# Sigmoid attention, ELU layer and expert choice on one core: batch 0's attention takes two chunks in one stretch of TensorE

## The chip, the cores and the metric

The kernel runs on one core of a Trainium2 chip. Five engines each run their own list of instructions in order and wait for one another through semaphores: TensorE (PE, with its weight loads as PEld), VectorE (DVE), ScalarE (ACT), GpSimd (POOL) and SyncE (SP), whose queue issues nearly all the transfers. The metric is the device time of one launch in microseconds (us); less is better.

## The reference

Four batches of sigmoid attention, an ELU layer and an expert-choice layer, one after the other:

```
q, k, v: (4, 12, 448, 64)
scores = q @ k.T / sqrt(64) - log(448)
x = (1 / (1 + exp(-scores))) @ v             # to (1792, 768)
h = x @ w_in                                 # (768, 2048)
x = where(h > 0, h, exp(min(h, 0)) - 1) @ w_out   # to (1792, 768)
# expert choice: 8 experts, 224 tokens each, by sorted gate logits
out[mask] = relu(x[mask] @ w1[e]) @ w2[e]
```

w_in and w_out come as 64-bit floats, the other inputs that matter here as 32-bit floats.

## The kernel before, in words

Every product of two fp32 matrices that must be exact is split: an operand x is held as h (rounded to the matmul format fp32r) and l = x - h, and three matmuls h\*h, h\*l, l\*h are added up. An operation on VectorE or ScalarE makes h (a copy, `hcopy`), and one on VectorE makes l (a subtraction, `lsub`).

**Attention** of a batch (`attention(b)`) goes by pairs of heads, six in a batch, and by chunks of 112 keys, four in a pair: 24 chunks. `scores(n)` is six matmuls of 64 rows into one of two twin tiles of PSUM, which are taken in turn (`twin_74` for even chunks, `twin_75` for odd ones in the order rows below). ScalarE then writes the sigmoid of the whole twin into a buffer `ad[n]`. `values(n)`, two matmuls with 64 output rows each, adds the chunk to the pair's sum in the one bank `bank_73`. `values` of a chunk comes `XLA` = 2 chunks after its scores. After a pair's fourth chunk the sum is split into h and l (`xs[b]`), and the next pair's first `values` has to wait for that, since it writes the same bank.

**Layer 1** (`layer1(b)`) computes, for each of 16 column blocks f of w_in, 18 matmuls of 128x128x448 (six row blocks c, one for each pair of heads, by three products) into one of three banks in turn (`bank_70` to `bank_72`). The block's ELU is two operations on ScalarE (exp and tanh), two on VectorE, and a split of the result. The second of the two on VectorE is the last that reads the bank. **Layer 2** (`layer2(b)`) adds 16 such blocks for each of six columns d of w_out, in two banks in turn (`bank_70`, `bank_71`), so that its first matmul needs `bank_70`, which block f = 15 held.

**Weights.** In batch 0, `weights` loads each block as 64-bit words into one of two arena tiles (`arena<-w_in`, 768 KB) and `join` makes 32-bit floats of it: one operation on ScalarE that reads the arena, then three on VectorE (`TENSOR_SCALAR`, and two `SCALAR_TENSOR_TENSOR` that read the arena). The joined block goes to memory for the later batches (`wcopy`) and is split into h and l; h and l have three buffers each.

**Order.** The order of instructions on every engine is fixed when the kernel is built, by a list scheduler (`Plan`). Each call adds an operation with a priority and modelled cost; `plan.unit()` binds several matmuls into one operation that nothing comes between; `plan.run()` then places operations one at a time on the engine where the model has the earliest start, and copies (`AV_`) go to ScalarE or VectorE as the model prefers. At run time each engine keeps its list, whatever the real times are, and so does SP's queue with its transfers.

Of the kernel before, what the change touches and what calls it, by code (L numbers as in the profile page):

```python
# [37 lines left out]
Z1R = 11648  # L38
FMAX = 3.4028234663852886e38
W0 = 11  # L40
AC0 = 1
AC1 = 2


# [246 lines left out]
def kernel(  # L291
# [34 lines left out]
    plan = Plan(nc)  # L326
# [62 lines left out]
    def hcopy(dst, src):  # L389
        AV_.copy(dst, src)  # L390

    def lsub(dst, src, h):
        V.tensor_tensor(out=dst, in0=src, in1=f32(h), op=ALU.subtract)
# [126 lines left out]
    def prep(g, st):  # L520
        x, vr = pairs[g]
        h, l = r_kqh(), r_kql()
        for c in (slice(0, S), slice(S, 2 * S)) if g == 0 else (slice(0, 2 * S),):
            hcopy(h[:, c], x[:, c])
            lsub(l[:, c], x[:, c], h[:, c])
        st[g] = (h[:, :S], l[:, :S], h[:, S:], l[:, S:], vr)
        load_pair(g + 2)

    def attention(b):


        st, ad = {}, {}
        n0, n1 = b * HP * C, (b + 1) * HP * C
        AC = AC0 if b == 0 else AC1
        acc = {}

        def scores(n):
            g, c = divmod(n, C)
            kh, kl, qh, ql, _ = st[g]
            ps = sc()  # L540
            for i, (w, m) in enumerate(((kh, qh), (kh, ql), (kl, qh))):
                for j in range(2):
                    o = slice(j * D, (j + 1) * D)
                    PE.matmul(ps[:CP, j, :S], w[o, c * CP:(c + 1) * CP], m[o], start=i == 0, stop=i == 2)
            return ps

        def values(n):
            g, c = divmod(n, C)
            if c == 0:
                acc[g] = av()  # L550
            v, s = st[g][4], ad.pop(n)
            for j in range(2):
                o = slice(j * D, (j + 1) * D)
                PE.matmul(acc[g][o, :S], v[:, c, o], s[:, j], start=c == 0, stop=c == C - 1)

        for n in range(n0, n1 + XLA, AC):
            new = [i for i in range(n, n + AC) if i < n1]
            old = [i for i in range(n - XLA, n - XLA + AC) if i >= n0]
            for i in new:
                g, c = divmod(i, C)  # L560
                if i == n0:
                    prep(g, st)
                if c == PP and g + 1 < (b + 1) * HP:
                    prep(g + 1, st)
            with plan.unit():
                pss = [scores(i) for i in new]
                if b:
                    for i in old:
                        values(i)
            if not b and old:  # L570
                with plan.unit():
                    for i in old:
                        values(i)
            for i, ps in zip(new, pss):
                ad[i] = r_s()[:CP]
                A.activation(ad[i], ps[:CP, :, :S], AF.Sigmoid, bias=bias_s[:CP], scale=QS)
            if old and old[-1] % C == C - 1:
                h, l = r_xH(), r_xL()
                ps = acc.pop(old[-1] // C)
                hcopy(h, ps[:, :S])  # L580
                lsub(l, ps[:, :S], h)
                xs[b].append((h, l))
# [104 lines left out]
    V.tensor_scalar(ident, pj, 0.0, None, op0=ALU.is_equal)  # L687
    plan.bias = BIAS[0]
    attention(0)
    for b in range(B):  # L690
        plan.bias = BIAS[1] if b == 0 else {}
        layer1(b)
        if b == 0:
            plan.dma(wg, w_gate.rearrange("(d p) e -> p d e", p=P))
            V.tensor_copy(wgs[:, :, :E], wg)
            lsub(wgs[:, :, E:], wg, wgs[:, :, :E])
            V.memset(wgp, 0.0)
            V.tensor_copy(wgp[:, :, :E], wg)
        plan.bias = BIAS[2] if b == 0 else {}
        if b + 1 < B:  # L700
            attention(b + 1)
        layer2(b)
# [403 lines left out]
```

## Time and profile before

| what | value |
| --- | --- |
| time, median of 3 runs | 1009.49 us (1008.43 to 1009.92) |
| the profiled execution's own time | 1010.62 us |
| its span, first to last instruction | 1008.8 us |
| PE busy | 976.4 us (97%) |
| DVE busy | 752.6 us (75%) |
| ACT busy | 445.8 us (44%) |
| DMA queue q1, share of 16 engines | 48.8% |

Busy is the time in which an engine ran instructions of work. The shares are means over a program of several stages: attention of batch 0 fills the first 48 us, its layer 1 runs to 121 us, beside the start of batch 1's attention, and the rest follows. A row of the timeline gives start, duration, engine, operation, result and operands, how many instructions were merged, and in brackets the idle time before with what ended it. The trace counts a `values` matmul as two.

### The profile page before, as it was taken

How to read it: one execution, taken by the hardware profiler on the slowest of the kernel's cores; microseconds unless marked ns; L12 is line 12 of the kernel's file. 1: busy time of each engine (PE TensorE's matmuls, PEld its weight loads, DVE VectorE, ACT ScalarE, POOL GpSimd, SP SyncE). 2: the span in 40 equal slices, each digit the busy share in tenths (PEclk: the TensorE clock that was granted, in tenths of full speed). 3: DMA queues.
4: the chain of work that ended last, by engine and by line, in shares of the span. 5: the costliest groups of instructions: out<-in, count | busy, mean ns of one | idle time of the engine just before them, and what ended most of it. 6: DMA issues, size and time to landing. Idle time of an engine off the chain costs nothing. (4 is left out here: it accounts for less than half of the span.)

```text
span 1008.8 us, 15529 instructions
## 1 busy us (share of the span) xinstructions
PE 976.4 (97%) x6039; PEld 811.5 (80%) x6039; DVE 752.6 (75%) x1335; ACT 445.8 (44%) x631; POOL 45.6 (5%) x42
## 2 busy tenths in 40 slices
PE   8999999998999999899999999999899999999997
PEld 3497666786886698777678898888899989989997
DVE  5899977769996445997434687788798899798861
ACT  6779856446564412675320342133433244342320
POOL 0000000000000000000000000010011111102000
PEclk9999999999999999999999999999899999999999
DMA  7856767866452366433124333375555547456820
GB/s 218 294 201 237 264 229 265 271 230 213 175 203 86 115 171 198 164 115 111 63 79 138 113 115 105 120 252 185 174 208 174 187 137 278 163 168 239 282 89 28
DMA packets 63562, 177.99 MB, mean 176 GB/s; under 512 B 6336, under 2 KB 28096, under 8 KB 60416
## 3 DMA queue, kind: packets, MB, share of 16 engines
q1 hardware_dynamic: 60832, 165.98, 48.8%
q0 software_dynamic: 2656, 11.01, 3.5%
q8 instruction: 47, 0.77, 0.3%
q14 instruction: 27, 0.22, 0.1%
HBM read 147.87 MB, written 29.10 MB: 175 GB/s over the span
## 5 line engine op out<-in xcount | busy, mean ns | idle before, releaser
L247 PE MATMUL bank<-zone_r 128*128 128x448 f32 (+1 forms) x3384 | 633.7, 343 | 12.9 <-DVE zone L247 10.1
L247 PEld LDWEIGHTS bank<-zone_r 128*128 128x128 f32 x3384 | 556.3, 191 | 79.5 <-issue 20.6
L247 DVE TENSOR_TENSOR zone_r<-zone,zone_r 128x768 fp32r<-128x768 f32 (+3 forms) x347 | 314.3, 918 | 34.9 <-ACT zone_r L247 28.3
L247 PE MATMUL twin<-zone_r 128*112 128x384 f32 (+2 forms) x1416 | 226.2, 354 | 3.3 <-ACT zone L247 3.3
L247 PEld LDWEIGHTS twin<-zone_r 128*112 128x112 f32 (+2 forms) x1416 | 187.0, 175 | 33.4 <-issue 15.6
L247 ACT ACTIVATE zone_r<-zone 128x768 fp32r<-128x768 f32 (+3 forms) x194 | 151.6, 795 | 123.2 <-PE bank L247 48.6
L247 ACT ACTIVATE zone<-bank 128x448 f32<-128x448 f32 x156 | 79.5, 542 | 187.2 <-PE bank L247 161.0
L247 DVE CAST zone_r<-zone 128x768 fp32r<-128x768 f32 (+3 forms) x153 | 84.9, 557 | 91.0 <-PE bank L247 69.5
L247 ACT ACTIVATE zone<-twin,bias_s 112x896 f32<-112x896 f32 x96 | 92.8, 1005 | 61.5 <-PE twin L247 61.2
L247 PE MATMUL bank<-zone 112*64 112x448 f32 x384 | 83.9, 553 | 0.9 <-DVE zone_r L247 0.9
L247 ACT ACTIVATE zone_r<-bank 128x448 fp32r<-128x448 f32 x62 | 33.5, 544 | 111.5 <-PE bank L247 111.2
L247 DVE SCALAR_TENSOR_TENSOR zone<-arena,zone 128x768 int32<-128x768 int32 (+1 forms) x56 | 59.8, 1068 | 1.0
L247 PEld LDWEIGHTS bank<-zone 112*64 112x64 f32 x384 | 22.8, 136 | 37.7 <-issue 33.8
L247 DVE TENSOR_TENSOR arena<-m,arena 128x896 bf16<-128x896 f32 (+1 forms) x35 | 51.0, 1457 | 0.0
L247 ACT ACTIVATE zone<-twin 112x384 f32<-112x384 f32 (+2 forms) x48 | 24.7, 536 | 50.3 <-DVE zone L247 20.0
L247 DVE SCALAR_TENSOR_TENSOR zone<-zone 128x448 f32<-128x448 f32 x64 | 39.5, 618 | 2.5 <-ACT zone L247 2.5
L247 DVE SCALAR_TENSOR_TENSOR zone<-zone,bank 128x448 f32<-128x448 f32 x64 | 39.4, 616 | 1.0
L891 POOL DMA_INDIRECT zone<-x2rows,idx x18 | 24.2, 1343 | 340.6 <-PE bank L247 234.8
L247 ACT ACT_TABLE_LOAD x29 | 37.2, 1283 | 3.3 <-PE bank L247 1.6
L247 DVE CAST zone_r<-bank 128x448 fp32r<-128x448 f32 x13 | 8.1, 623 | 36.1 <-PE bank L247 36.1
L247 DVE TENSOR_TENSOR zone_r<-bank,zone_r 128x448 fp32r<-128x448 f32 x45 | 27.5, 618 | 3.1 <-ACT zone_r L247 2.7
L247 ACT ACTIVATE zone<-arena 128x768 f32<-128x768 f32 (+1 forms) x28 | 28.1, 1004 | 2.2 <-DMA arena<-w_out 1.3
(106 smaller groups left out, 365.9 us busy)
## 6 DMA issues: line engine op xcount, KB each, us to landing
zone<-we SPq DMA_DIRECT2D x64, 768.0 KB, 5.7
zone<-wcopy SPq DMA_DIRECT2D x48, 384.0 KB, 3.0
zone<-wcopy SPq DMA_DIRECT2D x36, 512.0 KB, 3.3
arena<-w_in SPq DMA_DIRECT2D x16, 768.0 KB, 4.7
arena<-w_out SPq DMA_DIRECT2D x12, 1024.0 KB, 5.9
arena<-w_outT SPq DMA_DIRECT2D x12, 1024.0 KB, 7.1
x2rows<-zone SPq DMA_DIRECT2D x48, 224.0 KB, 3.8
zone<-kq SPq DMA_DIRECT2D x23, 448.0 KB, 3.4
```

The costliest lines, as they stand in the source:

```text
L247: fn = lambda: getattr(self.eng[e], name)(*args, **kw)
L891: plan.add([("G", 1.05, lambda: plan.eng["G"].indirect_dma_start(**kw))], [plan.region(x) for x in reads], [plan.region(x) for x in writes ...
```

## The change

`attention` takes AC = 2 chunks a step in batch 0 as well, where it took one; and the values of the two older chunks go into the same unit as the scores of the two new ones, where they had a unit of their own.

```
-AC0 = 1
 AC1 = 2
...
-        AC = AC0 if b == 0 else AC1
+        AC = AC1
...
             with plan.unit():
                 pss = [scores(i) for i in new]
-                if b:
-                    for i in old:
-                        values(i)
-            if not b and old:
-                with plan.unit():
-                    for i in old:
-                        values(i)
+                for i in old:
+                    values(i)
```

Since the list scheduler starts from other units, the order on every engine changes up to some 260 us of the program. Three places follow; in them `zone`, `zone_r` and `arena` are buffers, and x6 is six instructions in a row.

ScalarE, from the sigmoid of chunk 3 on (`zone<-twin,bias_s` is a sigmoid, even chunks from twin_74; `zone<-arena_77` is ScalarE's part of the join of w_in block 0). Before:

```order
L247 ACTIVATE zone<-twin_75,bias_s 112x896
L247 ACTIVATE zone<-twin_74,bias_s 112x896
L247 ACTIVATE zone<-twin_75,bias_s 112x896
L247 ACTIVATE zone_r<-bank_73 128x448
L247 ACTIVATE zone<-twin_74,bias_s 112x896
L247 ACTIVATE zone<-twin_75,bias_s 112x896
L247 ACTIVATE zone<-twin_74,bias_s 112x896
L247 ACTIVATE zone<-arena_77 128x768
L247 ACTIVATE zone<-twin_75,bias_s 112x896
```

The same stretch of ScalarE now, from the sigmoid of chunk 3 to that of chunk 10:

```order
L246 ACTIVATE zone<-twin_75,bias_s 112x896
L246 ACTIVATE zone<-twin_74,bias_s 112x896
L246 ACTIVATE zone<-twin_75,bias_s 112x896
L246 ACTIVATE zone<-twin_74,bias_s 112x896
L246 ACTIVATE zone<-arena_77 128x768
L246 ACTIVATE zone<-twin_75,bias_s 112x896
L246 ACTIVATE zone_r<-zone 128x768
L246 ACTIVATE zone<-twin_74,bias_s 112x896
L246 ACTIVATE zone<-twin_75,bias_s 112x896
L246 ACTIVATE zone<-twin_74,bias_s 112x896
```

The join stood behind the sigmoid of chunk 8 and now stands behind that of chunk 6, ahead of chunk 7's; the split of the attention's first sum (`zone_r<-bank_73`) has left ScalarE for VectorE, and the copy of the joined weights (`zone_r<-zone`) now stands ahead of the sigmoid of chunk 8.

SP's queue from the transfer of the fifth pair's v and of w_in block 0 on. Before:

```order
L278 DMA zone<-vP 112x512
L278 DMA arena_77<-w_in 128x1536
L278 DMA zone<-kq 128x896
L278 DMA zone<-vP 112x512
L278 DMA arena_78<-w_in 128x1536
L278 DMA wcopy<-zone 128x768
```

And now:

```order
L277 DMA zone<-vP 112x512
L277 DMA arena_77<-w_in 128x1536
L277 DMA zone<-kq 128x896
L277 DMA wcopy<-zone 128x768
L277 DMA zone<-vP 112x512
L277 DMA arena_78<-w_in 128x1536
```

The write-back of the joined block 0 has come ahead of the load of block 1; in both orders that load stands behind v of the sixth pair.

TensorE between the last values of batch 0's attention (`bank_73`) and block f = 7 of layer 1 (18 matmuls into one of bank_70 to bank_72 are one block f). Before:

```order
L247 MATMUL bank_73<-zone 64x448 x8
L247 MATMUL bank_70<-zone_r 128x448 x15
L247 MATMUL bank_71<-zone_r 128x448 x18
L247 MATMUL bank_72<-zone_r 128x448 x18
L247 MATMUL bank_70<-zone_r 128x448 x18
L247 MATMUL bank_71<-zone_r 128x448 x18
L247 MATMUL bank_72<-zone_r 128x448 x18
L247 MATMUL bank_70<-zone_r 128x448 x18
L247 MATMUL bank_71<-zone_r 128x448 x18
```

And now, where 45 of the 54 matmuls of blocks 0 to 2 stand among the attention's chunks already:

```order
L246 MATMUL bank_73<-zone 64x448 x4
L246 MATMUL twin_74<-zone_r 112x448 x6
L246 MATMUL twin_75<-zone_r 112x448 x6
L246 MATMUL bank_70<-zone_r 128x448 x3
L246 MATMUL bank_71<-zone_r 128x448 x3
L246 MATMUL bank_72<-zone_r 128x448 x3
L246 MATMUL twin_74<-zone_r 112x448 x6
L246 MATMUL twin_75<-zone_r 112x448 x6
L246 MATMUL bank_73<-zone 64x448 x4
L246 MATMUL bank_70<-zone_r 128x448 x18
L246 MATMUL bank_71<-zone_r 128x448 x18
L246 MATMUL bank_72<-zone_r 128x448 x18
```

The last pair of heads' share of blocks 0 to 2 and the first four chunks of batch 1 stand ahead of block 3 now. From here to the first matmul of layer 2 the old order holds five pairs of scores and four pairs of values of batch 1, the new one four and three. Counted over the whole program, TensorE's list falls from 466 stretches of matmuls of one shape to 457.

## Rows read from the trace of the kernel before

**Rows 1.** Three stretches: busy us (instructions) of each engine, granted clock, DMA share, GB/s
```profile
0.00:57.70 57.70, 53.09 (x300) 27.03 (x301) 39.24 (x70) 41.05 (x50) 0.43 (x5) 1.00 0.79 257
57.70:128.30 70.60, 65.21 (x333) 50.94 (x331) 68.38 (x101) 59.11 (x84) 0.00 (x0) 1.00 0.67 228
128.30:160.00 31.70, 31.61 (x166) 22.89 (x166) 22.95 (x27) 19.36 (x22) 0.00 (x0) 0.95 0.69 242
```

**Rows 2.** Timeline of VectorE at two of the ELUs of layer 1
```profile
53.21 0.55 DVE L247 TENSOR_SCALAR zone<-zone 128x768 int32<-128x768 int32 x1
...
55.67 0.62 DVE L247 SCALAR_TENSOR_TENSOR zone<-zone 128x448 f32<-128x448 f32 x1
56.20 0.95 DVE L247 TENSOR_TENSOR zone_r<-zone,zone_r 128x768 fp32r<-128x768 f32 x1
57.07 0.61 DVE L247 SCALAR_TENSOR_TENSOR zone<-zone,bank 128x448 f32<-128x448 f32 x1
...
127.72 0.62 DVE L247 SCALAR_TENSOR_TENSOR zone<-zone,bank 128x448 f32<-128x448 f32 x1
```

**Rows 3.** Timeline of TensorE, the start of layer 2
```profile
128.39 8.51 PE L247 MATMUL bank<-zone_r 128*128 128x448 f32 x33 [2.68 <-DVE zone L247]
```

**Rows 4.** Timeline of TensorE in and behind batch 0's attention
```profile
6.48 1.48 PE L247 MATMUL twin<-zone_r 64*112 64x448 f32 x12
...
13.55 0.87 PE L247 MATMUL twin<-zone_r 64*112 64x448 f32 x6
...
15.25 1.49 PE L247 MATMUL twin<-zone_r 64*112 64x448 f32 x12
16.68 1.72 PE L247 MATMUL bank<-zone 112*64 112x448 f32 x8
18.33 0.86 PE L247 MATMUL twin<-zone_r 64*112 64x448 f32 x6
...
20.81 0.97 PE L247 MATMUL bank<-zone 112*64 112x448 f32 x4
...
23.01 0.87 PE L247 MATMUL twin<-zone_r 64*112 64x448 f32 x6 [0.44 <-ACT zone L247]
...
48.27 29.39 PE L247 MATMUL bank<-zone_r 128*128 128x448 f32 x141
```

**Rows 5.** Timeline of SP's queue: transfers issued
```profile
15.36 0.33 SPq L278 DMA_DIRECT2D zone<-vP  x1
15.74 0.42 SPq L278 DMA_DIRECT2D arena<-w_in  x1
...
21.82 0.33 SPq L278 DMA_DIRECT2D zone<-vP  x1
22.20 0.42 SPq L278 DMA_DIRECT2D arena<-w_in  x1
25.07 0.33 SPq L278 DMA_DIRECT2D wcopy<-zone  x1
```

**Rows 6.** Timeline of ScalarE around its first join
```profile
16.23 1.91 ACT L247 ACTIVATE zone<-twin,bias_s 112x896 f32<-112x896 f32 x2 [0.26 <-PE twin L247]
19.29 1.01 ACT L247 ACTIVATE zone<-twin,bias_s 112x896 f32<-112x896 f32 x1 [1.16 <-PE twin L247]
21.16 0.90 ACT L247 ACTIVATE zone<-arena 128x768 f32<-128x768 f32 x1 [0.86 <-DMA arena<-w_in]
21.96 0.99 ACT L247 ACTIVATE zone<-twin,bias_s 112x896 f32<-112x896 f32 x1
```

**Rows 7.** Timeline of ScalarE behind batch 0's attention
```profile
51.46 0.84 ACT L247 ACTIVATE zone_r<-zone 128x768 fp32r<-128x768 f32 x1 [2.52 <-PE bank L247]
52.21 0.91 ACT L247 ACTIVATE zone<-arena 128x768 f32<-128x768 f32 x1
53.14 1.28 ACT L247 ACT_TABLE_LOAD   x1
54.43 0.98 ACT L247 ACTIVATE zone<-bank 128x448 f32<-128x448 f32 x2
```

**Rows 8.** Who TensorE waited for between 6 and 48 us: us, times, longest
```profile
PE twin L247 <- ACT zone L247: 0.9, 2, 0.5
PE bank L247 <- DVE zone_r L247: 0.9, 2, 0.5
```

**Rows 9.** TensorE alone, 2 us each: busy us, granted clock, DMA share, GB/s
```profile
126.00:128.00 2.00, 0.00 (x0) 1.00 0.55 191
130.00:132.00 2.00, 2.00 (x7) 0.50 0.97 317
```

## The prediction

> **What bounds the kernel now.** I read the page's busy shares first: TensorE is busy 97% of the span, so at first sight anything that shortens its list shortens the program. But the change touches only the first stages, so I split those with the view by stretches [rows 1]. Its second stretch, from the release of layer 1's block 0 to that of block 15, shows VectorE busy 68.38 of 70.60 us and TensorE 65.21: there VectorE sets the pace. The two ends of this stretch are the second and third of the ELU rows on VectorE that matter: the operation that last reads block 0's bank starts at 57.07 and ends at 57.7, and block 15's starts at 127.72 and ends at 128.3 [rows 2]. Layer 2's first matmul starts at 128.39, right behind it, after 2.68 us in which TensorE waited for VectorE [rows 3]; it needs the bank that block 15 held. From there TensorE is busy 31.61 of 31.70 us [rows 1]. So the chain is: batch 0's attention, then VectorE's joins and ELUs up to 128.3, then TensorE. A gain on TensorE ahead of 128 us reaches the end only if VectorE comes sooner, and what TensorE leaves undone there is paid later in full. In the first stretch VectorE is busy 39.24 of 57.70 us; those 18.5 us of idle time are what can grow or shrink.
>
> **The stretches saved.** A chunk alone takes TensorE 1.70 us (13.55 to 15.25) and two chunks in one stretch 3.08 (15.25 to 18.33) [rows 4]. Two alone would be 3.40, so 0.32 for two stretches, 0.16 each. The new list has 9 stretches fewer in the whole program: 1.4 us less work. By this alone the time would be 1009.49 - 1.4 = 1008.1. The Trainium skill (TensorEngine Tiling (Array Packing), Tiling Modes, Key Properties) says why: a change of the tiling mode drains TensorE. That the order of the other engines changes with it stands on no such page, and the following comes from rows.
>
> **The first join.** In the old order the values of chunk 3 end at 15.3; then SP can load the fifth pair's v (15.36) and w_in block 0 (15.74) [rows 5]. ScalarE waits for that load and starts its join at 21.16 [rows 6]: 5.4 us from issue to use. There it costs little, since the join stands behind the sigmoid of chunk 8, and TensorE waits only 0.44 us, at 23.01 [rows 4]. In the new order four single chunks become two pairs ahead of this point, 0.64 less: values end at 14.6, the load is issued at 15.1, and lands at 20.5. The join now stands behind the sigmoid of chunk 6. Queued behind it on ScalarE is chunk 7's sigmoid, which runs from 21.3 (0.80 from join to sigmoid, 21.16 to 21.96 [rows 6]) to 22.3. The scores of chunk 9 write the twin that it reads. TensorE is through with chunk 8's scores at 14.6 + 3.1 + 0.8 = 18.5, and stands in a unit that nothing passes: 3.8 us of waiting.
>
> **The loop that follows.** Values of chunks 6 and 7 then end at 24.7, where they ended at 21.8 [rows 4]. The sixth pair's v waits for them, and the load of w_in block 1 stands behind it: 25.1 instead of 22.20 [rows 5]. It lands at 30.5, and its join stands ahead of chunk 11's sigmoid. In the same way TensorE's first matmuls of layer 1 wait for the split of pair 1's sum, which VectorE now does behind join 0 and its lsub, until 26.9: 1.5 us. Join 1 holds chunk 13's scores by 1.0. Three further places, traced with the same prices, hold TensorE by 0.9 (the split of pair 2), 1.3 (that of pair 3, behind two joins) and 0.2. The sum is 8.7 us, against 1.8 now (0.9 each for ScalarE and VectorE [rows 8]). Batch 0's attention ends at 6.48 + 12 pairs of 3.08 + 45 matmuls of layer 1 at 0.208 (29.39 for 141 [rows 4]) + 6 stretches of 0.16 + 8.7 = 62.6. The old order has done the same work at 48.27 + 42 x 0.208 = 57.0.
>
> **VectorE at block 0.** From 62.6 TensorE does chunks 24 and 25 of the next attention (1.4) and the last nine matmuls of blocks 0 to 2, until 66.0. Only then are their weight buffers free, and ScalarE copies blocks 3 to 5 (0.75 each, 51.46 to 52.21), does two joins (0.93 each), a sigmoid, a table load (1.29) and exp and tanh (0.98) [rows 7]: done at 72.1. VectorE's list ahead of the ELU is three lsubs (0.87, 56.20 to 57.07) and two joins (2.46 each, 53.21 to 55.67) [rows 2], which end at 72.9; with the ELU's two operations block 0 is released at 74.1, 16.4 us later than at 57.7. Of these VectorE works 8.2: two joins more ahead of that point (eight instead of six, 4.9), a lsub (0.9) and four copies of attention sums that ScalarE did (0.6 each, 2.4). The other 8.2 us are new idle time.
>
> **VectorE to block 15.** Up to the release of block 15 VectorE's list holds 170 instructions in both orders, of nearly the same kinds. So what came earlier is missing later: 70.6 - 8.2 = 62.4 us from block 0 to block 15, the old idle time of 2.2 kept. 74.1 + 62.4 = 136.5: the start of layer 2 moves by 8.2. TensorE isn't the bound there: 13 blocks of 18 x 0.208 are 48.7 us, and two pairs 6.2, so it could be through at 129.
>
> **What TensorE leaves undone.** Ahead of layer 2 it now does one pair of chunks of batch 1 less. That pair (3.1 us) lay in waiting time; now it lies behind 128 us, where TensorE has none. The switches saved lie ahead of layer 2, hidden by VectorE: worth nothing.
>
> **Sum.** 8.2 + 3.1 = 11.3. Against the profiled execution: span 1008.8 + 11.3 = 1020.1, its own time 1010.62 + 11.3 = 1021.9. That execution is 1.1 over the median of 1009.49, so I forecast 1020.8.
>
> **What is not in the rows** is a load of w_in in the new order. The old loads took 5.4 with the DMA engines 0.79 busy in that stretch. The loads of blocks 0, 1 and two later ones lie on the loop; each us sooner or later on all four moves the attention's end by up to 4, and VectorE's idle time with it: 1016.8 to 1024.8. I keep 5.4, the only row.
>
> **Rivals.**
> *VectorE makes good part of it* (15%): the later joins fall into waits that are there anyway, only the first 3.8 us count, of which 1.8 replace old waits. Layer 2 starts 0 to 3 later; with the pair, 1012.6 to 1015.6. For it: VectorE has 18.5 us idle in the first stretch. Against: each of its waits there is for a load that now comes later.
> *The clock* (13%): between 126 and 128 TensorE did nothing, and between 130 and 132 the granted clock was 0.50, the lower level of 1.2 GHz [rows 9]; the 33 matmuls from 128.39 took 8.51 us [rows 3] instead of 6.9, 1.6 more. If the wait of 3.8 us at 18.5 does the same, the chunks behind it are slower, all of the loop comes 1.6 later, and with a second such place near 70 us the time is 1022.4 to 1028. The Trainium skill (TensorE: Matmul & The Clock Gate, Why this matters for your kernels) warns of idle gaps between bursts of matmuls for that reason; the trace agrees, with the 0.50 above.
> *No change that can be measured* (8%; within 0.2%, 2 us, which is about what runs of this kernel can tell): layer 2 starts 1 to 5 us sooner, and the pair eats it.
> *Faster* (9%): the join doesn't hold the sigmoid. This decides at ScalarE's first join: were block 0 in the arena when chunk 6's sigmoid ends at 16.4, TensorE would not wait, and would save the 1.8 us of old waits with the 1.4 of stretches: 1006.3. It needs 1.3 us from issue to use, against 5.4 in the row, and VectorE's idle time must also fall by more than the pair's 3.1 before anything reaches the end.
>
> **The numbers.** Forecast 55% (1015.6 to 1024.8 by itself, the loads' bounds and the absorbed part). Slower than 1011.5: 0.55 + 0.15 + 0.13 = 0.83; same 0.08, faster 0.09. Leaving out those two and the top of the clock's case, the range is 1012 to 1027.
>
> **What would show it.** Right: ScalarE's join of block 0 some 4 us behind chunk 6's sigmoid, and a wait of TensorE for ScalarE of 3 to 4 us near 19; w_in block 1 issued near 25; batch 0's last values near 62; block 0 released near 74, block 15 near 136; a wait of some 7 us ahead of layer 2. Wrong: if the load lands before chunk 6's sigmoid is done, or if VectorE reaches block 15 by 128 in spite of a later block 0, because it idles less than 2 us in between or ScalarE's four table loads fewer (7 instead of 11 ahead of block 15) were what held it.

## The result, and the profile after

The changed kernel takes 1021.24 us (median of 3 runs, 1020.77 to 1024.02) against 1009.49: 1.0132 times as long, with a 95% interval of 1.0102 to 1.0161. (The ratios in this document are worked out over the runs of both kernels; the two medians by themselves give 1.0116.) Its profiled execution took 1020.77 us with a span of 1019.0. The forecast of 1020.8 us held, and so did its sign and its range of 1012 to 1027.

TensorE's timeline of the changed kernel, in the attention and at the start of layer 2, answers to [rows 3] and [rows 4]:

```profile
18.31 0.88 PE L246 MATMUL twin<-zone_r 64*112 64x448 f32 x6
22.85 0.87 PE L246 MATMUL twin<-zone_r 64*112 64x448 f32 x6 [3.66 <-ACT zone L246]
23.64 3.24 PE L246 MATMUL bank<-zone 112*64 112x448 f32 x8
...
65.70 1.72 PE L246 MATMUL bank<-zone 112*64 112x448 f32 x8
...
74.36 1.03 PE L246 MATMUL twin<-zone_r 64*112 64x448 f32 x6 [2.69 <-ACT zone L246]
75.32 3.19 PE L246 MATMUL bank<-zone 112*64 112x448 f32 x8
...
140.57 4.82 PE L246 MATMUL bank<-zone_r 128*128 128x448 f32 x12 [2.70 <-DVE zone L246]
```

The wait forecast at 18.5 for 3.8 us is there: 3.66 us at 22.85, for ScalarE. Behind it eight matmuls take 3.24 us that take 1.72 in [rows 4], and the clock view of the same kernel (TensorE busy, granted clock, DMA share, GB/s) shows the lower level of 1.2 GHz, behind the waits at 22.85, 74.36 and 140.57:

```profile
20.00:22.00 2.00, 0.00 (x0) 1.00 0.54 194
...
24.00:26.00 2.00, 2.00 (x8) 0.50 0.34 137
...
76.00:78.00 2.00, 2.00 (x8) 0.50 0.27 106
140.00:142.00 2.00, 1.43 (x4) 0.50 0.67 240
```

Next ScalarE's timeline of the changed kernel, for [rows 6]:

```profile
21.01 0.89 ACT L246 ACTIVATE zone<-arena 128x768 f32<-128x768 f32 x1 [3.84 <-DMA arena<-w_in]
21.80 1.00 ACT L246 ACTIVATE zone<-twin,bias_s 112x896 f32<-112x896 f32 x1
...
55.56 0.92 ACT L246 ACTIVATE zone<-arena 128x768 f32<-128x768 f32 x1 [3.45 <-DMA wcopy<-zone]
...
71.72 1.70 ACT L246 ACTIVATE zone<-arena 128x768 f32<-128x768 f32 x2
...
83.70 0.89 ACT L246 ACTIVATE zone<-arena 128x768 f32<-128x768 f32 x1
```

SP's queue, the loads of w_in, for [rows 5]:

```profile
27.30 0.42 SPq L277 DMA_DIRECT2D arena<-w_in  x1
...
62.91 0.37 SPq L277 DMA_DIRECT2D arena<-w_in  x1
...
77.08 0.37 SPq L277 DMA_DIRECT2D arena<-w_in  x1
```

VectorE's timeline, the ELUs of blocks 0 and 15, for [rows 2]:

```profile
78.06 0.62 DVE L246 SCALAR_TENSOR_TENSOR zone<-zone,bank 128x448 f32<-128x448 f32 x1
...
139.81 0.61 DVE L246 SCALAR_TENSOR_TENSOR zone<-zone,bank 128x448 f32<-128x448 f32 x1
```

The first join (21.01) stands ahead of chunk 7's sigmoid (21.80), and block 1's load is issued at 27.30. Block 0's bank is released at 78.06 + 0.62 = 78.7, block 15's at 139.81 + 0.61 = 140.4, and layer 2 starts at 140.57, 12.2 us later than at 128.39 [rows 3].

Where the time went shows best in stretches that end at the same point of the program, by the view by stretches (length, then busy us and instructions of PE, PEld, DVE, ACT, POOL). Of each kernel one row runs to the release of block 15, one from there to the end of the first 2232 matmuls (with the short wait behind them), one over both, and the last is the stretch of a gather behind the last layer 2. The changed kernel has one more at the head, to the release of block 0. The kernel before:

```profile
0.00:128.33 128.33, 118.30 (x631) 77.97 (x631) 107.66 (x170) 100.18 (x134) 0.43 (x5) 1.00 0.73 241
128.33:441.10 312.77, 305.36 (x1601) 239.00 (x1601) 227.76 (x312) 155.93 (x209) 0.00 (x0) 0.99 0.57 191
0.00:441.10 441.10, 423.66 (x2232) 316.97 (x2232) 335.42 (x480) 256.11 (x342) 0.43 (x5) 0.99 0.62 205
695.40:719.00 23.60, 19.60 (x157) 18.80 (x157) 13.57 (x42) 5.60 (x9) 3.73 (x4) 0.86 0.49 160
```

The changed kernel:

```profile
0.00:78.68 78.68, 63.88 (x337) 31.08 (x337) 47.55 (x81) 44.27 (x52) 0.43 (x5) 0.96 0.62 203
0.00:140.42 140.42, 120.35 (x611) 78.68 (x611) 108.22 (x170) 95.53 (x128) 0.43 (x5) 0.96 0.65 215
140.42:454.00 313.58, 309.62 (x1621) 240.29 (x1621) 231.54 (x316) 155.49 (x208) 0.00 (x0) 0.98 0.58 192
0.00:454.00 454.00, 429.98 (x2232) 318.97 (x2232) 339.76 (x485) 251.02 (x335) 0.43 (x5) 0.98 0.60 200
708.33:727.50 19.17, 16.73 (x157) 15.95 (x157) 13.02 (x41) 5.56 (x9) 3.73 (x4) 1.00 0.60 197
```

Up to block 15 VectorE does the same 170 instructions, 107.66 and 108.22 us of work; its idle time grows from 20.7 to 32.2. At the end of the 2232 matmuls the changed kernel is 12.9 behind: 6.6 in TensorE's idle time (24.02 for 17.44) and 6.3 in its busy time, which holds the slower clock. The last row then gives 4.4 back, and the last 116 us of the program take 1.5 more. I don't put the 4.4 down to the change: TensorE waits there for rows gathered from memory, and over the kernels of this study that wait was anything from 0 to 3.5 us, and 1.8 and 0 in two that share one order. So the profiled spans lie 10.2 apart where the medians lie 11.75 apart.

### The profile page after: what moved, and what is told of

Its sections match the earlier page's. It is cut to its first block, busy times and chain, and to the rows that moved or that the text cites. A ratio compares the mean times of both kernels' runs of the same rounds, so it can differ in the third digit from the quotient of the medians.

```text
span 1019.0 us, 15535 instructions
## 1 busy us (share of the span) xinstructions
PE 981.4 (96%) x6039; PEld 812.0 (80%) x6039; DVE 756.3 (74%) x1340; ACT 440.9 (43%) x624; POOL 47.1 (5%) x42
## 5 line engine op out<-in xcount | busy, mean ns | idle before, releaser
L246 ACT ACTIVATE zone<-twin,bias_s 112x896 f32<-112x896 f32 x96 | 92.4, 1003 | 64.8 <-PE twin L246 64.6
L246 ACT ACTIVATE zone_r<-bank 128x448 fp32r<-128x448 f32 x57 | 30.7, 544 | 115.7 <-PE bank L246 111.1
L246 DVE CAST zone_r<-bank 128x448 fp32r<-128x448 f32 x18 | 11.2, 622 | 45.9 <-PE bank L246 45.9
```

The lines of the kernel that those rows point to most:

```text
L246: fn = lambda: getattr(self.eng[e], name)(*args, **kw)
```

## The experiments

Each ratio is to the kernel before, run on the same chip in the same group of runs, with its 95% interval.

**The joins held back.** My theory: the joins that stand too early in the attention cost the time. The planner may place the first five only behind the sigmoids that they stood behind in the old order (`hold` adds a predecessor):

```diff
...
+        joins.append(plan.ops[-1])
+        if len(joins) <= 5:
+            hold(joins[-1], sigs[(8, 12, 16, 19, 23)[len(joins) - 1]])
...
```

> The changed kernel, with the first five joins of w_in held in the list scheduler behind the sigmoids that they followed in the old order (chunks 8, 12, 16, 19, 23). Theory (the joins ahead of sigmoids cause the loss, not the two-chunk stretch): TensorE's wait of 3.66 us at chunk 9's scores falls under 0.8, block 1 of w_in is issued near 22 instead of 27.3, batch 0's attention with its filler ends by 62 instead of 67.3, and the time is 1004 to 1011. Rival (the stretch of two chunks itself costs, since it waits for two sigmoids): TensorE's waits in the attention stay at 6 us or more, and the time stays at 1018 to 1022.

Measured: 1027.31 us, ratio 1.0150 (1.0110 to 1.0189), slower than either side expected. TensorE's timeline of this kernel:

```profile
27.81 0.87 PE L246 MATMUL twin<-zone_r 64*112 64x448 f32 x6 [1.70 <-ACT zone L246]
...
57.37 1.72 PE L246 MATMUL bank<-zone 112*64 112x448 f32 x8
...
141.04 1.12 PE L246 MATMUL twin<-zone_r 64*112 64x448 f32 x6 [4.77 <-ACT zone L246]
...
147.46 3.68 PE L246 MATMUL bank<-zone_r 128*128 128x448 f32 x15
```

The attention got as good as hoped: the last values start at 57.37 instead of 65.70. But the planner's new order brings a wait of 4.77 us for a sigmoid of batch 1, and layer 2 starts at 147.46. An attention that ends 8 us sooner was worth nothing here, under an order that had changed everywhere.

**The parts of the change.** Two kernels take one half of the change each; both cuts show them as edits of the changed kernel. First two chunks a step, with the values in a unit of their own:

```diff
-                for i in old:
-                    values(i)
+                if b:
+                    for i in old:
+                        values(i)
+            if not b and old:
+                with plan.unit():
+                    for i in old:
+                        values(i)
```

> Half of the change: two chunks of scores in one stretch for batch 0, but the older two chunks' values in a unit of their own, as before. The scheduler then puts the first join behind chunk 8's sigmoid again and leaves five pairs of scores ahead of layer 2. Theory: no wait above 1 us near 18 to 23, block 1 of w_in issued near 22, time 1006 to 1011. Rival (the stretch of two chunks' scores costs by itself): waits and time as in the changed kernel, 1018 to 1022.

The other, one chunk a step with the values in the unit of the scores:

```diff
+AC0 = 1
...
-        AC = AC1
+        AC = AC0 if b == 0 else AC1
```

> The other half: one chunk a step as before, but its values in the unit of the scores. The first join stands behind chunk 7's sigmoid, ahead of chunk 8's. Theory: chunk 10's scores, which write the twin that chunk 8's sigmoid reads, wait 1 to 1.5 us near 22, less than the 3.66 of the changed kernel since the join stands one sigmoid later; time 1005 to 1013, since seven pairs of scores lie ahead of layer 2. Rival (only stretches of two chunks cost): no such wait, 1008.5 to 1010.5 as before the change.

Measured: 1015.34 us, ratio 1.0050 (1.0032 to 1.0067), and 1022.27 us, ratio 1.0124 (1.0095 to 1.0152). The first keeps less than half of the loss, the second about all of it, and both missed every range expected. The second has few waits in its attention (1.0 us for ScalarE and 1.9 for VectorE), and is as slow as the changed kernel. Its longest wait stands elsewhere, on TensorE's timeline ahead of layer 2:

```profile
144.94 1.46 PE L247 MATMUL twin<-zone_r 64*112 64x448 f32 x6 [7.80 <-ACT zone L247]
```

So each edit of a unit gives a whole new order, with its own waits far behind the edit.

**Work in the wait.** The changed kernel's own order on every engine, with 19 matmuls of unused data between the scores of chunks 8 and 9:

```diff
+FILL = 19
...
-                pss = [scores(i) for i in new]
+                pss = [scores(new[0])] if new else []
+                if new and new[0] == 8:
+                    for _ in range(FILL):
+                        plan.group.append((0.0, lambda: plan.eng["PE"].matmul(
+                            banks[2][:, :S], idle[:, :P], idle[:, :S], start=True, stop=True),
+                            [plan.region(idle)], [plan.region(banks[2])], 1))
+                pss += [scores(i) for i in new[1:]]
```

> The changed kernel with 19 dummy matmuls of 128x448 into an unused bank between the scores of chunks 8 and 9, where TensorE waits 3.66 us; the order on the other engines stays the same. Theory (the halved clock behind that wait made the loop later than the prediction had it): granted clock 1.00 from 22 to 28, the eight values behind it take 1.72 instead of 3.24, block 1 of w_in is issued near 25.7 instead of 27.3, block 0's bank is released near 77 instead of 78.7, and the time falls by 1 to 2 us to 1019.2 to 1020.2. Rival (the clock's loss is absorbed in other waits): the release and the time stay within 0.5 of 78.7 and 1021.2.

Measured: 1015.29 us, ratio 1.0063 (1.0043 to 1.0083), 6 us less than the changed kernel by the medians and 7 by the ratios, more than expected. TensorE's timeline of this kernel:

```profile
19.69 3.77 PE L569 MATMUL bank<-idle 128*128 128x448 bf16 x19
...
24.18 1.72 PE L247 MATMUL bank<-zone 112*64 112x448 f32 x8
...
138.25 3.95 PE L247 MATMUL bank<-zone_r 128*128 128x448 f32 x12 [2.66 <-DVE zone L247]
```

The clock view of the two us in which the changed kernel had 0.50:

```profile
24.00:26.00 2.00, 2.00 (x13) 1.00 0.32 129
```

The eight matmuls behind the wait take 1.72 us again, at a granted clock of 1.00. The Trainium skill (TensorE: Matmul & The Clock Gate, Why this matters for your kernels) advises against idle gaps between bursts of matmuls; the trace agrees, with 1.00 for 0.50. Layer 2 starts 2.3 us sooner and the 2232 matmuls end at 449.3 instead of 454.0. So the clock behind this one wait costs 1.5 us where it falls and 2.3 at the start of layer 2. The other 2.4 us of the 4.7 arise behind two waits that both kernels have. At the start of layer 2 twelve matmuls take 4.82 us behind 2.70 in the changed kernel, and 3.95 behind 2.66 here. The second place is on TensorE's timelines near 428 us, first of the changed kernel and then of this one:

```profile
428.67 2.69 PE L246 MATMUL bank<-zone_r 128*128 128x448 f32 x9 [2.51 <-DVE zone L246]
425.52 2.06 PE L247 MATMUL bank<-zone_r 128*128 128x448 f32 x9 [2.69 <-DVE zone L247]
```

Behind waits of nearly one length the clock fell in one trace and not, or not as far, in the other (0.93 from 428 to 454 us, 1.00 from 425 to 449.3), so no run shows that the fill earned these 2.4 us. The profiled execution, 1012.44 us, is also the fastest of its seven. The rest, up to 7, lies in a stretch in which the gather differs, and I leave it open.

**One exchange.** The changed kernel with chunk 7's sigmoid ahead of the first join on ScalarE, and nothing else moved: the order is found as before, and two instructions are exchanged as it is written out.

```diff
-            [a for a in op.alts if a[0] == e][0][2]()
+            seq.append((op, [a for a in op.alts if a[0] == e][0][2]))
...
+        seq.insert(j, seq.pop(s7))
+        for op, fn in seq:
+            fn()
```

> The changed kernel with one exchange on ScalarE: chunk 7's sigmoid stands ahead of the first join instead of behind it; every other row of every engine keeps its place. In the changed kernel's trace TensorE waits 3.66 us at 22.85 for that sigmoid and the 8 values behind the wait take 3.24 us at half the clock; its first 2232 matmuls end at 454.0 us (441.1 in the kernel before). By the prediction's step (the sigmoid behind the join is what holds TensorE) the wait at 22.85 goes, no wait over 1.5 us takes its place, the granted clock stays at 1.00 there, the 2232 matmuls end 3 to 5 us earlier (449 to 451) and the time is 1015 to 1018 us. By the rival (TensorE's own row is as early as ScalarE's: four matmuls of block 0 of layer 1 stand behind the values of chunks 6 and 7, and their weights are not split before about 25.5 to 26.5 us, since the transfer lands at 21.0) the wait only moves: 3 to 5 us ahead of those four matmuls, at about 22 to 26 us, the clock falls as before, and the time is within 1.5 us of the changed kernel's (1019.5 to 1022.5).

Measured: 1023.35 us, ratio 1.0147 (1.0120 to 1.0174), 0.9 us above the rival's range. The rival was right about what happens: the wait moves to the first matmuls of layer 1, on TensorE's timeline:

```profile
24.88 0.68 PE L253 MATMUL bank<-zone_r 128*128 128x448 f32 x2 [3.99 <-ACT zone_r L253]
...
28.11 2.58 PE L253 MATMUL twin<-zone_r 64*112 64x448 f32 x12
```

It waits 3.99 us, and the clock falls again (0.50 from 26 to 32 us; 2.58 us for twelve matmuls of scores, 1.48 elsewhere). In the new order ScalarE and TensorE both come to block 0 before its weights are there.

**The planner's landing times.**

```diff
+LATE = 1.5
...
-                op.end = dma + 1.0
+                op.end = dma + 1.0 + getattr(op, "late", 0.0)
...
-            plan.dma(x[:, :n], src)
+            plan.dma(x[:, :n], src, LATE if r < KF else 0.0)
```

> The changed kernel, with the planner told that batch 0's w_in transfers land 1.5 us later than it had assumed; it makes a whole new order, in which two more chunks stand ahead of the first matmuls of layer 1 and chunk 7's sigmoid stands ahead of the first join. If the early joins of the attention are the loss, TensorE's waits between 6 and 70 us sum to under 4 us (9.0 in the changed kernel), its first 2232 matmuls end at 444 to 450 us and the time is 1010 to 1016 us. By the rival (the attention's waits are one part; each new order brings other waits in batch 0's layer 1 and in batch 1, as in the run with the joins held) the attention is as good, but the 2232 matmuls end at 452 us or later and the time is 1017 to 1026 us.

Measured: 1017.75 us, ratio 1.0098 (1.0061 to 1.0135), inside the rival's range. Neither side was right about the attention: the waits in it (7.7 us, 9.0 in the changed kernel) only moved, as TensorE's timeline shows. ScalarE still comes to the first join 4.2 us ahead of its load.

```profile
23.99 1.46 PE L247 MATMUL twin<-zone_r 64*112 64x448 f32 x6 [2.70 <-ACT zone L247]
27.44 1.46 PE L247 MATMUL twin<-zone_r 64*112 64x448 f32 x6 [1.99 <-ACT zone L247]
```

**The change under the old order.** All these mix the stretches with a new order, so here the order of the kernel before is written into the changed kernel (ORDER, one word for each operation with its engine):

```diff
+ORDER = """
...
+        place = {t[:-1]: (i, t[-1]) for i, t in enumerate(ORDER.split())}
...
+            op = self.ops[heapq.heappop(heap)[1]]
+            e = place[op.tag][1]
```

> The change without the new order that it brings: batch 0's attention takes two chunks and the values behind them in one stretch, as in the changed kernel, but the planner's result is replaced by the order of the kernel before, written into the kernel. Every other operation keeps its old place and engine; each merged stretch stands where the last of its old parts stood, and a sigmoid whose scores it moved stands right behind it. If the stretches themselves cost nothing and the loss is the new order (first join and first matmuls of layer 1 placed ahead of the transfer that they need, and the waits and the halved clock behind that), the first 2232 matmuls end within 3 us of the kernel before's 441.1 us and the time is 1006 to 1012 us. By the rival (two chunks in one stretch hold the sigmoids back, and TensorE then waits for score banks whatever the order) TensorE waits over 5 us in 6 to 60 us and the time is 1015 us or more.

Measured: 1010.02 us, ratio 1.0021 (1.0003 to 1.0039). The stretches by themselves cost about 0.2% and no more than 0.4; the other 1.1% is the order that the planner makes of them. The waits in the attention alone are not it: TensorE waits 5.0 us there from 6 to 60 us, where it waited 1.8 before (3.5 of them for ScalarE), nearly as much as the rival had set for a slow kernel, and hardly any time is lost. ScalarE's timeline at the ninth join:

```profile
73.66 0.90 ACT L449 ACTIVATE zone<-arena 128x768 f32<-128x768 f32 x1
```

The stretch up to the release of block 15:

```profile
0.00:130.80 130.80, 118.88 (x631) 78.84 (x631) 107.92 (x170) 100.42 (x134) 0.43 (x5) 0.99 0.70 235
```

VectorE is idle for 22.9 us there: 2.2 more than before, where the changed kernel has 11.5 more.

**Which part of the new order.** Orders can now be joined. First the order of the joins held back, up to the last values of batch 0, and from there on the changed kernel's (an order text in place of the one above):

> The changed kernel with two planner results joined: up to the last values of batch 0's attention the order is the one of the run with the five joins held, from there on it is the changed kernel's own, operation by operation. In the run with the joins held the attention waited 2.2 us for ScalarE (6.1 in the changed kernel) and ended at 59.1 us (67.35), and the time was lost behind it. If the attention's waits and the halved clock behind them are what the changed kernel loses, this one ends its first 2232 matmuls at 446 to 450 us (454.0) and takes 1011 to 1017 us. By the rival (what follows the attention in the changed kernel's order is bound by VectorE or by its own waits, and takes the lead back) they end at 452 us or later and the time is 1018 to 1023 us.

Measured: 1020.26 us, ratio 1.0132 (1.0105 to 1.0160): nothing is won. Then, on top of this, the seventh and eighth join behind the ELUs of blocks 0 to 2 (ScalarE's rows of the joined order and of this one):

```diff
-ACTIVATE zone<-arena_77 128x768
-ACTIVATE zone<-arena_78 128x768
 ACT_TABLE_LOAD
 ACTIVATE zone<-bank_70 128x448 x2
 ...
 ACTIVATE zone<-bank_72 128x448 x2
+ACTIVATE zone<-arena_77 128x768
+ACTIVATE zone<-arena_78 128x768
```

> The joined order of the last run, with one more move: the seventh and eighth join (two operations on ScalarE, six on VectorE) stand behind the exponentials and the ELUs of blocks 0 to 2 instead of ahead of them. In the last run the attention ended at 58.9 us instead of 67.35 and nothing was won: block 0 was released at 76.8 (78.7), since ScalarE waited 5.96 us for the transfer of those joins with block 0's exponentials behind them; VectorE was idle for 32.5 of the 141.0 us up to block 15's release (20.7 of 128.3 in the kernel before, 32.2 of 140.4 in the changed one), with 107.7 to 108.5 us of work in each. If VectorE's idle time ahead of block 15 is the loss, and those two joins are what keeps it there once the attention is early, block 0 is released at 66 to 69 us, VectorE's idle time falls to 24 to 28 us, block 15 is released at 132 to 137 us and the time is 1010 to 1017 us. By the rival (VectorE loses as much later, at the joins moved) block 15 stays at 139 us or later and the time is 1018 to 1023 us.

and that move alone in the changed kernel's order:

> The changed kernel's own order with that move alone: the seventh and eighth join behind the exponentials and ELUs of blocks 0 to 2. Here the attention ends at 67.35 us, and ScalarE's three copies at 71.8. If VectorE's idle time is the loss, this wins nothing by itself: the idle time lies ahead of 70 us, and the joins and the ELUs only change places behind it. Block 0 is released at 73 to 75 us (78.7), but block 15 still at 138 to 141 us, and the time is 1017.5 to 1023 us. By the rival (those two joins alone are the loss) block 15 is released by 135 us and the time is 1010 to 1016 us.

Measured: 1017.92 us, ratio 1.0087 (1.0063 to 1.0111), and 1025.21 us, ratio 1.0162 (1.0138 to 1.0186). With both, block 15 came when expected (135.5) and the time is 1 us over its range. The move alone is not neutral: block 15 comes 4.8 us later than in the changed kernel and the time is outside both ranges, though its interval overlaps the changed kernel's.

In the joined order TensorE has its 8 us and gives them all back in one wait (TensorE's timeline):

```profile
57.16 1.72 PE L449 MATMUL bank<-zone 112*64 112x448 f32 x8
...
76.93 17.23 PE L449 MATMUL bank<-zone_r 128*128 128x448 f32 x72 [10.97 <-DVE zone L449]
```

SP's queue, the seventh and eighth load:

```profile
59.99 0.37 SPq L480 DMA_DIRECT2D arena<-w_in  x1
...
62.24 0.38 SPq L480 DMA_DIRECT2D arena<-w_in  x1
```

ScalarE's timeline, the seventh and eighth join:

```profile
69.85 1.68 ACT L449 ACTIVATE zone<-arena 128x768 f32<-128x768 f32 x2 [5.96 <-DMA arena<-w_in]
```

The stretch up to the release of block 15:

```profile
0.00:140.99 140.99, 117.62 (x611) 79.86 (x611) 108.47 (x170) 95.65 (x128) 0.43 (x5) 0.94 0.64 215
```

It waits 10.97 us for VectorE to release block 0, whose exponentials stand behind two joins on ScalarE; these wait 5.96 us for loads that were issued as a pair. The order text also has the load of block 7 ahead of that of block 6, and block 6 joined first, so that ScalarE waits for the load issued second. With the joins moved on top of it, ScalarE's ninth join:

```profile
78.28 0.89 ACT L449 ACTIVATE zone<-arena 128x768 f32<-128x768 f32 x1 [4.36 <-DMA arena<-w_in]
```

and the stretch up to block 15:

```profile
0.00:135.54 135.54, 116.74 (x611) 79.92 (x611) 108.29 (x170) 95.32 (x128) 0.43 (x5) 0.96 0.67 223
```

What these seven have in common is the pace of the joins. Starts of ScalarE's second, fifth, seventh and ninth join, and the release of block 15 by VectorE:

| kernel | join 2 | join 5 | join 7 | join 9 | block 15 | block 15 less join 9 |
| --- | --- | --- | --- | --- | --- | --- |
| before | 27.76 | 45.90 | 60.12 | 71.13 | 128.3 | 57.2 |
| the change, old order | 28.88 | 48.43 | 62.80 | 73.66 | 130.8 | 57.2 |
| joined order and joins moved | 28.54 | 53.09 | 67.55 | 78.28 | 135.5 | 57.3 |
| work in the wait | 31.17 | 53.21 | 69.39 | 81.39 | 138.1 | 56.7 |
| changed | 32.08 | 55.56 | 71.72 | 83.70 | 140.4 | 56.7 |
| joined order | 30.20 | 55.71 | 69.85 | 84.27 | 141.0 | 56.7 |
| joins moved alone | 32.18 | 53.82 | 77.21 | 87.98 | 145.2 | 57.2 |

Whatever is done ahead of it, block 15 comes 56.7 to 57.3 us behind the ninth join, in all kernels that have either old or new order behind it, also in the one with the exchange and the two with another bank below. (In the four that were planned anew it is 60.9 to 67.7, with waits of their own there, as the 4.77 and 7.80 us above.) Behind the seventh join it is 68.0 to 71.1. So the loss up to block 15 is complete when the ninth join starts; that the joins' pace makes it is what I take from this, and no run changes that pace alone. Nor does block 15 settle the whole time: it comes sooner with the joined order and the joins moved (135.5) than with work in the wait (138.1), and the ratios don't follow it (1.0087 and 1.0063, with intervals that overlap).

There are two arena tiles, so the ninth load can be issued only when the seventh join is through. SP's queue in the kernel before, the eighth and ninth load:

```profile
56.21 0.37 SPq L278 DMA_DIRECT2D arena<-w_in  x1
...
64.60 0.37 SPq L278 DMA_DIRECT2D arena<-w_in  x1
```

The ninth is issued at 64.60 there and at 77.08 in the changed kernel. The old order runs the joins one by one, and its loads come at most 8.4 us apart (the two rows above). The new one runs them in pairs (55.56 and 57.29, then two from 71.72), the loads wait for the pair, and come up to 14.2 us apart (62.91, 77.08).

**A version that beats both.** Layer 2 starts in bank 0, the one that block 15 has just used. One index of its ring lets it start in bank 1, first in the kernel before and then in the changed one:

```diff
-        m3 = Ring(banks[:MM - 1])
+        m3 = Ring(banks[MM - 2::-1])
```

> The kernel before, with one number changed: layer 2 begins its ring of two PSUM banks with bank 1 in place of bank 0, the one that block 15 of layer 1 has just used. If layer 2 waits only for that bank's release by VectorE, its first matmul moves from 128.4 to about 125.7 us, the halved clock behind the wait (about 1.4 us) goes, the later layer 2 starts gain 2 to 3 us each where they wait for the same (417.39 us, 2.85 us of wait), and the time is 1000 to 1006 us. By the rival (VectorE bounds these stretches, so TensorE gives the time back ahead of the first product that needs the late block, or at the start of the next batch's layer 1) the time is within 2 us of the kernel before's, 1007 to 1012 us.

> The same one number in the changed kernel. If the change's loss sits in TensorE's and VectorE's lost time in the attention, and not in the wait at layer 2's start, this gains what the same edit gains in the kernel before, and the two stay 10 to 14 us apart: 1011 to 1018 us. If the loss is that layer 2 must wait for block 15's release by a VectorE that runs late, this edit gives most of it back and the two come within 6 us of each other.

Measured: 1002.35 us, ratio 0.9934 (0.9912 to 0.9955), and 1016.64 us, ratio 1.0089 (1.0062 to 1.0117). TensorE's timeline of the first of them:

```profile
124.95 2.79 PE L247 MATMUL bank<-zone 112*64 112x448 f32 x8
127.68 8.78 PE L247 MATMUL bank<-zone_r 128*128 128x448 f32 x42
```

The wait of 2.68 us [rows 3] is gone. Layer 2 still starts at 127.68 and not at the 125.7 expected, since the clock is low (0.50 from 124 to 126 us) behind a short wait at 123.64 (2.79 us for the eight values). I have not split the 7 us over the later layers. They aren't shown to be the bank's alone: from some 136 us on the planner's order differs on every engine here too, and no run gives layer 2 the other bank under the old order. The two stay 14.3 us apart: the wait at the start of layer 2 is a toll that both kernels pay, and not the loss of the change.

## Why the prediction came out right, point by point

**The chain: right.** Attention, then VectorE up to block 15, then TensorE. VectorE's work up to there is the same to 0.6 us and its idle time grows by 11.5, which is nearly all of the 12.1 us by which block 15 comes later.

**The first join: right as a wait, half right as a cause.** 3.66 us for 3.8, at the place forecast. But the exchange of two instructions shows that the join ahead of the sigmoid isn't all that holds TensorE: without it, its own list asks for block 0 as early and waits as long.

**The loop: right in its waits, short by the clock.** From 6 to 62 us TensorE waits 6.1 us for ScalarE and 2.9 for VectorE, 9.0 for the 8.7 forecast. Block 1's load is issued at 27.30 (25.1), the attention ends at 65.70 + 1.72 = 67.4 (62.6; its terms add up to 62.5): 1.5 us of that is the halved clock behind the first wait, the rest I have not split.

**VectorE at block 0: the step that was mis-sized.** It put 8.2 us of more work and 8.2 of new idle time ahead of block 0's release. The work measured 8.3 (47.55 for 39.24 [rows 1]); the idle time grew by 12.7, from 18.5 to 31.1. So block 0 is released at 78.7 and not at 74.1, nearly as much too late as the attention's end. (By the step's own prices ScalarE, counted from 66.0, is done at 73.3; its 72.1 fits a start at 64.8, when the first of the three weight buffers is free.)

**VectorE to block 15: right.** 61.7 us for the 62.4 forecast, and layer 2 starts 12.2 later instead of 8.2. One of the signs fails here: the wait ahead of layer 2 is 2.70 us and not some 7, since TensorE comes to it only at 137.9 and not at 129. And the 62.4 is no fixed distance from block 0 that another order would keep. In the joined order block 0 is released at 76.8 and block 15 at 141.0; with the joins moved, at 64.9 and 135.5: 11.9 us at the one end, 5.5 at the other, as two joins (4.9 us of VectorE's work) then lie on the other side of block 0. What keeps its distance over these kernels is the ninth join.

**What TensorE leaves undone: wrong.** The pair's work is there behind block 15: TensorE runs 20 matmuls more up to the end of the 2232 and is busy 309.62 us for 305.36 (a slower clock is part of it). But "behind 128 us, where TensorE has none", namely no waiting time, was read from the 31.7 us behind 128.3 alone [rows 1]. Up to 441.1 the kernel before idles 7.4 us on TensorE (312.77 - 305.36), among them 1.15 at 244.18 and 2.38 at 250.51; the changed kernel idles 4.0, and these two waits are gone. So the stretch lasts 313.6 us for 312.8, 0.8 more and not 3.1.

**The sum: close by luck.** A term 3.9 us too small and one 2.3 too large offset: 12.1 + 0.8 = 12.9 for 8.2 + 3.1 = 11.3. The medians say 11.75, and the interval of the ratio allows 10 to 16.

**The rivals.** The clock, at 13%, was partly there as well as the forecast case: it fell behind waits at 22.85, 74.36 and 140.57. Its price on the first of them is 2.3 us at the start of layer 2, about a fifth of the loss, so it belonged in the sum. "Partly absorbed" and "faster" had no trace in the changed kernel. "No change" is what the same edit gives under the old order, for a reason that none of the rivals held: the stretches are harmless and the planner is not.

Still open is which of the planner's choices comes first. The early join and the attention's waits were undone, and one pair of joins was moved, without winning the whole back; only the old order did that. No run takes the pairs of joins apart, or loads blocks 6 and 7 in their order, with the rest kept.

## What to carry to other kernels

Where a scheduler makes the order, an edit of one unit is an edit of the whole program: run it once under the old order, written out, before the edit itself is blamed or praised. Look for the event that keeps a fixed distance to the end of the stage over several variants (here the ninth join), as the event next to the end may move freely: it tells up to where to look, and not yet the cause. And look at which buffer a stage begins in: beginning with one that is free earlier, with the new order that this brought, was worth 0.66%, 6.7 us, where the prediction put the stretches saved at 1.4 us of TensorE's work.

## What was not expected of the hardware

The joined order issues two loads of w_in 2.25 us apart (59.99 and 62.24). The view of that tile from 55 to 75 us has both:

```profile
DMA to landing us min/median/max: 7.0/7.3/7.5
```

A load by itself took 5.4 [rows 5, 6]. ScalarE starts at 69.85, when the second has landed (62.24 + 7.5), though the first was there at 67.0.

The clock behind a wait of TensorE isn't the same each time: one order, with waits of 2.51 to 2.70 us at two places, took 4.82 and 2.69 us for the same matmuls behind them in one trace, 3.95 and 2.06 in another.

The gather behind the last layer 2 is ready 0 to 3.5 us late from kernel to kernel. In the kernel before it is the long wait that also lowers the clock: 157 matmuls and their waits take 23.60 us there at a granted clock of 0.86, and 19.17 at 1.00 in the changed kernel. A difference of two single profiles holds such draws; here it hid 4.4 of 12.9 us.
